# Four chunk pairs by seven products, one ReLU for a score pair, and a few squares and one form moved

## The chip, the cores and the metric

The kernel runs on one core of one Trainium2 chip. The core has a matrix engine (TensorE, called PE in the profile), a vector engine (VectorE, DVE), a scalar engine (ScalarE, ACT), GpSimd (POOL) and SyncE (SP), which here only issues DMAs. PE writes its results to PSUM, eight banks of 128 x 512 float32 values; ACT and DVE carry them from there to SBUF, the main on-chip memory. The metric is the device time of one execution in microseconds (us), as the median of several runs.

## The reference

Two computations follow each other. Attention without a softmax, over 8 batches of 3072 tokens, model width 256, key width 64:

```python
scores = (1.0 / S) * np.matmul(z, z.transpose(0, 2, 1))
attn = np.maximum(scores, 0.0) ** 2
x = u * np.matmul(attn, v)
```

Then a feed-forward part ("ff" below) on all 24576 tokens, with inner width 1024:

```python
h1 = x @ w1
h2 = x @ w2
out = np.maximum(h1, h2) @ w_out
```

The score matrix is symmetric, since queries and keys are the same z. In the ff, max(h1, h2) = relu(h1 - h2) + h2, so the kernel needs one inner product with the difference w1 - w2, a ReLU, and one linear term x @ (w2 @ w_out), whose matrix it works out once (`W2o_sb`).

## The kernel before, in words

**Tiling.** The 3072 tokens of a batch are 24 tiles of 128, in 6 groups of 512. Two groups make a couple, so a batch has 3 couples (c = 0, 1, 2). Scores are held in bf16 blocks of 512 x 512 (`Block`, `blk` in the profile). Only blocks on and above the diagonal are computed; the others are made by DMA transposes on SP (`mirror`, line 289, and for the blocks on the diagonal line 271). DMA transposes also turn z and u (lines 170, 220).

**Scores.** `score_pair` (from line 229) computes two tiles at a time: two matmuls of 64 rows each, side by side on the two row halves of PE (line 244), into two PSUM banks. Each half leaves its bank by a ReLU of 128 x 512 on ACT (line 258). Some steps later `finish` squares the pair, 128 x 1024, on DVE (line 268) or on ACT (line 266). Blocks on the diagonal of later batches ("triangles") are computed only from the diagonal on and squared half by half (line 264). A list of numbers in the loop over couples says which pairs of a couple ACT squares; the last two pairs of most couples are `late`: their squares wait for a Q token of the ff that follows, on ACT.

**Attention by seven products.** For a couple, attention times v is a product of 2 x 2 blocks of blocks. It is done by a scheme with seven products instead of eight (`product`, line 1202 for the matmuls), whose left factors are sums and differences of score blocks ("forms", 128 x 2048 each, DVE, line 343) and whose right factors are sums and differences of v tiles (`vt`, lines 200 to 203). The products run in two lanes, one on each row half of PE, 84 steps for a couple. Where an accumulator passes from one half to the other, a no-operation on POOL relays the semaphore. The score pairs of the next couple are spread between the steps (`at_step`), 14 for a couple.

**Feed-forward by seven products.** After the attention of couple i comes the ff of couple i-1 (`ff_by_seven`; plain `ff` for the first two couples). The 1024 inner columns are 8 chunks of 128. Chunk n and chunk n + 4 with the two token groups again make a 2 x 2 product. Three of the four pairs (x, y, z) take seven products P1 to P7 (line 607), with forms of the weights (`wT_sb`) and of the tokens (`token_forms`, lines 521 to 524); the fourth pair of chunks is done plainly (N tokens, line 569, two matmuls for each chunk and group). P1 is copied: where a bank is idle that was last filled whole, ACT copies it into a second PSUM bank (line 611) and P2 adds to it there ("seeded"; then a ReLU on ACT, line 582, makes the result); where not, to SBUF (line 615), and the sum is made by a custom operation on DVE that adds and clips (line 619). P6 and P5, which add up in P1's bank, are copied to SBUF (line 615); P3 leaves by a ReLU, P7 and P4 by the custom operation.

**What sets the order.** Each engine runs its own instructions in the order of the program. The order of an ff is written out by hand as a string of tokens (`FF_ORDER`, `FF_ORDER_MID` for c = 1 of batches 1 to 6, `FF_ORDER_LAST`): P1x is a product, N10 a plain chunk, O0z1 the outer product of group 0 with chunk z1 (four matmuls of 256 columns, line 552), L0a half of the linear term (four as well), E0 the way out of group 0 (line 649), Q a late square, T the next of the tasks handed over: a sum left from attention, and the forms for the next attention, two for each block of the couple, in the order of the blocks. A task's place in the string is thus its place in DVE's queue. Four PSUM banks (`mm0` to `mm3`) serve scores and inner products in turn (`idle_banks`), four are accumulators.

Of the kernel before, what the change touches and what calls it, by code (L numbers as in the profile page):

```python
# [12 lines left out]
def kernel(  # L13
# [10 lines left out]
    nc = tc.nc  # L24
    fp32 = mybir.dt.float32
# [33 lines left out]
    gpool = ctx.enter_context(tc.tile_pool(name="gpool", bufs=8))  # L59
    opool = ctx.enter_context(tc.tile_pool(name="opool", bufs=4))  # L60
    mm_psum = ctx.enter_context(tc.tile_pool(name="mm_psum", bufs=1, space=bass.MemoryType.PSUM))
    acc_psum = ctx.enter_context(tc.tile_pool(name="acc_psum", bufs=1, space=bass.MemoryType.PSUM))

# [3 lines left out]
    idle_banks = [f"mm{n}" for n in range(4)]  # L67
# [3 lines left out]
    def mm_tile(shape, dtype, name, hold=False, seeded=False, full=False):  # L71
        tag = next((t for t in idle_banks if t in whole), None) if seeded else idle_banks[0]
        if tag is None:
            return None, None
        idle_banks.remove(tag)
        if not hold:
            idle_banks.append(tag)
        if not seeded:
            (whole.add if full else whole.discard)(tag)
        return mm_psum.tile(shape, dtype, name=name, tag=tag), tag  # L80
# [149 lines left out]
    def score_pair(b, g, m, dve_half=None, halves=False, act=False):  # L230
# [8 lines left out]
        s_ps = []  # L239
        for h in range(2):  # L240
            rows = ds(h * R, R)
            q = z_at(b, g * G, h)
            s_ps.append(mm_tile([P, GW], fp32, "s_ps", full=not lo[h])[0])
# [9 lines left out]
        for h in range(2):  # L253
            s, o = s_ps[h][:, lo[h] :], r[:, tiles[h] - k, lo[h] :]
            if h == dve_half:
                nc.vector.tensor_single_scalar(out=o, in_=s, scalar=0.0, op=ALU.max)  # L256
            else:
                nc.scalar.activation(o, s, AF.Relu)  # L258
# [211 lines left out]
    def gate(b, g, hs):  # L470
# [13 lines left out]
    NP = 3  # L484
    FORM_CHUNKS = tuple((n, KF // 2 + n) for n in range(NP))
    PLAIN_CHUNKS = tuple(n for n in range(KF) if n not in sum(FORM_CHUNKS, ()))
    FF_ORDER = (
        "T P1z T N10 N11 L1a P6z P2z L0b N01 T O11 P5z T P1x O0z1 N00 P3z O10 P2x L0a P7z P1y O0z2 P6x O00 T P6y P4z P2y O01 P5x P5y P7x O1z1 P7y P3x Q O0x1 P3y T O1z2 P4y O1x2 O0x2 O0y1 P4x O0y2 O1y2 O1y1 O1x1 L1b Q E0 E1 T"
# [3 lines left out]
        "T T P1x T N00 T N10 T L0a P6x P1z L1a P2x L0b T P5x O00 P2z O0x1 P6z T N01 P7x P3x O10 P5z T P1y O0z1 O0x2 P3z O1x2 T T P6y T P4x T P2y N11 O01 P5y P7z P7y O0y1 O1x1 T Q P3y O0z2 O11 P4y P4z O1y2 Q O0y2 T E0 O1z2 O1y1 O1z1 T T T L1b T T E1"  # L492
# [34 lines left out]
    def ff_by_seven(b, c, tasks, last=False):  # L527
# [3 lines left out]
        homes = [Block() for n in range(3)]  # L531
# [760 lines left out]
```

## Time and profile before

| what | value |
|---|---|
| median of 3 runs | 894.4 us (892.91 to 895.82) |
| the profiled execution | 894.84 us |
| its span, first to last instruction | 892.8 us |
| TensorE's granted clock | 0.999 |
| PE busy | 885.2 us, 99% |
| DVE busy | 764.9 us, 86% |
| ACT busy | 735.4 us, 82% |
| POOL busy | 97.7 us, 11% |
| mean share of DMA engines on the hardware queue q1 | 73.9% |
| attention's matmuls (line 1202) | 2144 + 1560, 376 ns each |
| products in the ff (lines 607 and 569) | 379 ns each |

Lengths of single matmuls overlap: PE starts the next long before one has ended, so counts times lengths exceed the span. The span is 0 to 892.8 us; a row such as "213.74 0.39 PE L607 ..." starts at 213.74 us and lasts 0.39. In brackets stands how long the engine had been idle and what ended the wait. L607 is line 607 of the kernel before. In a table by stage each row is one stretch of the span; behind the bar of each engine stand its busy time and number of instructions, and at the end the granted clock and the load of the DMA engines.

### The profile page before, as it was taken

The page shows a single profiled execution, that of the slowest core. Times are in us where ns is not written, and L with a number is a line of the kernel's source. Part 1 is how long each engine was busy: PE and PEld are TensorE (multiplying, and loading weights), DVE is VectorE, ACT ScalarE, POOL GpSimd, SP SyncE. Part 2 cuts the span into 40 slices and gives each one's busy share as a digit, 9 for nine tenths or more (in the row PEclk, how much of TensorE's full clock was granted, in tenths as well). Part 3 has the DMA queues.
Part 4 walks back from the last instruction along what each step waited for, and adds up shares of the span by engine and source line. Part 5 has one row for each costly group of instructions (what it writes and reads, how often), then busy time and mean ns, then how long its engine had stood idle before and what let it go on. Part 6 is the DMA issues. An engine that isn't in the chain of part 4 may idle for free.

```text
span 892.8 us, 19566 instructions
## 1 busy us (share of the span) xinstructions
PE 885.2 (99%) x7458; PEld 505.5 (57%) x7458; DVE 764.9 (86%) x1201; ACT 735.4 (82%) x1366; POOL 97.7 (11%) x176
## 2 busy tenths in 40 slices
PE   9999999999999999999999999999999999999997
PEld 4555555565565555655656556566465564655655
DVE  6897887889988899798998899988898889987755
ACT  7978888788888888888888889888889888894554
POOL 3222100111002010020101101011100110000000
PEclk9999999999999999999999999999999999999999
DMA  9999999989899889998999999999989999998302
GB/s 179 250 224 197 201 198 146 205 145 197 168 178 185 175 139 161 191 151 165 173 168 203 153 183 160 149 198 134 212 150 144 189 134 205 144 150 158 80 1 95
DMA packets 396014, 148.10 MB, mean 166 GB/s; under 512 B 361264, under 2 KB 375856, under 8 KB 395920
## 3 DMA queue, kind: packets, MB, share of 16 engines
q1 hardware_dynamic: 373488, 119.32, 73.9%
q0 software_dynamic: 22288, 27.40, 22.6%
q8 instruction: 58, 0.95, 0.4%
q14 instruction: 36, 0.29, 0.1%
q10 hardware_dynamic: 144, 0.13, 0.0%
HBM read 59.77 MB, written 25.17 MB: 95 GB/s over the span
## 4 chain that ended last, share of the span: by engine, by line
PE 98%; DVE 1%; DMA 1%; issue 0%; ACT 0%; DVEq 0%
PE acc L1202 45%; PE acc L552 21%; PE d_ps L607 11%; PE s_ps L244 7%; PE acc L305 4%; PE d_ps L569 4%; PE acc L733 2%; PE d_ps L711 2%; DMA blk<-blk 1%; PE acc L892 0%; PE tpz L129 0%; DVE h_sb L1097 0%; PE w2o_ps L1000 0%; PE acc L675 0%; DVE blk L268 0%
## 5 line engine op out<-in xcount | busy, mean ns | idle before, releaser
L1202 PE MATMUL acc<-blk,v_sb 64*128 64x512 bf16 x2144 | 386.9, 376 | 0.0
L258 ACT ACTIVATE blk<-s_ps 128x512 bf16<-128x512 f32 (+1 forms) x584 | 287.4, 554 | 62.9 <-PE s_ps L244 60.5
L343 DVE TENSOR_TENSOR blk<-blk,blk 128x2048 bf16<-128x2048 bf16 x260 | 313.0, 1220 | 18.4 <-DMA blk<-blk 11.4
L1202 PE MATMUL acc<-blk,vt 64*128 64x512 bf16 x1560 | 316.3, 376 | 0.0
L1202 PEld LDWEIGHTS <-v_sb 64*128 64x128 bf16 x2144 | 152.0, 94 | 126.0 <-issue 5.0
L552 PE MATMUL acc<-w_out_sb,g_sb 128*128 128x256 bf16 x1400 | 190.3, 273 | 0.0
L552 PEld LDWEIGHTS <-g_sb 128*128 128x128 bf16 x1400 | 136.9, 98 | 56.1 <-DVE g_sb L619 0.6
L1202 PEld LDWEIGHTS <-vt 64*128 64x128 bf16 x1560 | 123.8, 94 | 75.5
L582 ACT ACTIVATE g_sb<-d_ps 128x512 bf16<-128x512 f32 x212 | 120.1, 600 | 9.0 <-PE d_ps L607 7.8
L244 PE MATMUL s_ps<-zT 64*128 64x512 bf16 (+3 forms) x672 | 125.5, 357 | 0.5 <-DVE r_sb L256 0.3
L619 DVE CUSTOM_DVE_ANT_0 g_sb<-blk,d_ps 128x512 bf16<-128x512 f32 x133 | 88.7, 684 | 36.4 <-PE d_ps L607 23.7
L268 DVE TENSOR_TENSOR blk<-blk 128x1024 bf16<-128x1024 bf16 x134 | 89.2, 686 | 19.9 <-ACT blk L258 19.9
L266 ACT ACTIVATE blk<-blk 128x1024 bf16<-128x1024 bf16 x78 | 82.3, 1055 | 0.9
L615 ACT COPY blk<-d_ps 128x512 f32<-128x512 f32 x133 | 76.6, 588 | 6.7 <-PE d_ps L607 3.7
L1097 DVE TENSOR_TENSOR h_sb<-h_sb,acc 128x512 f32<-128x512 f32 x89 | 58.9, 684 | 24.0 <-PE acc L1202 16.0
L186 POOL DMA_DIRECT2D v_sb<-in_v_dram x90 | 48.5, 557 | 272.6 <-PE acc L1202 216.5
L607 PE MATMUL d_ps<-blk,wT_sb 128*128 128x512 bf16 x198 | 68.4, 379 | 0.3 <-DVE g_sb L619 0.3
L473 DVE SCALAR_TENSOR_TENSOR xT<-h_sb,uT 128x512 bf16<-128x512 f32 x96 | 61.3, 689 | 2.1 <-DMA uT<-un 2.1
L649 ACT COPY o_sb<-acc 128x512 f32<-128x512 f32 x86 | 48.2, 587 | 14.5 <-PE acc L552 12.0
L244 PEld LDWEIGHTS <-zT 64*128 64x128 bf16 x672 | 35.7, 94 | 37.6 <-issue 0.4
L1101 ACT COPY h_sb<-acc 128x512 f32<-128x512 f32 x66 | 38.9, 590 | 19.3 <-PE acc L1202 17.8
L611 ACT COPY d_ps<-d_ps 128x512 f32<-128x512 f32 x65 | 37.8, 581 | 16.9 <-PE d_ps L607 16.9
(91 smaller groups left out, 782.4 us busy)
## 6 DMA issues: line engine op xcount, KB each, us to landing
out_dram<-o_sb SPq DMA_DIRECT2D x95, 256.0 KB, 3.0
un<-in_u_dram POOLq DMA_DIRECT2D x44, 256.0 KB, 5.3
v_sb<-in_v_dram POOLq DMA_DIRECT2D x84, 128.0 KB, 6.6
blk<-blk SPq DMA_TRANSPOSE x240, 5.1
zn<-in_z_dram POOLq DMA_DIRECT2D x18, 128.0 KB, 4.7
blk<-in_u_dram SPq DMA_DIRECT2D x4, 512.0 KB, 4.5
v_sb<-in_v_dram POOLq DMA_DIRECT2D x6, 256.0 KB, 6.2
blk<-in_moe_w_dram SPq DMA_DIRECT2D x2, 512.0 KB, 4.3
```

The source lines that it names most:

```text
L244: nc.tensor.matmul(s_ps[h][:, lo[h] :], zT[rows, z_at(b, blk * G + tiles[h], h), :], zT[rows, q + lo[h] // P : q + G, :].rearrange("p t c ...
L258: nc.scalar.activation(o, s, AF.Relu)
L266: nc.scalar.activation(both, r, AF.Square)
L268: nc.vector.tensor_mul(both, r, r)
L343: op(*((by_key(x) if mixed else x.ap) for x in blocks))
L473: lambda dc=dc: nc.vector.scalar_tensor_tensor(out=x[:, dc, :].rearrange("p (t r) -> p t r", r=P), in0=hs[dc].rearrange("p (t r) -> p t r" ...
L552: nc.tensor.matmul(o_ps[key][:, t % 2, :], x[:, ts(t, P)], w, start=first, stop=not left[key] and t % 2 == 1, skip_group_check=last,)
L582: nc.scalar.activation(g, ps, AF.Relu)
L607: nc.tensor.matmul(ps, w, x, start=first, stop=ends, skip_group_check=True)
L615: nc.scalar.copy(u_[k, name], ps)
L619: nc.vector._custom_dve(TENSOR_ADD_SAT, out=g, in0=u_[k, with_], in1=ps, s0=float("inf"), s1=0.0)
L1202: mm = nc.tensor.matmul(a.out(acc[name]), w()[rows], a.moving(rows, j), start=first, stop=left[name] == 0, skip_group_check=True,)
```

## The change

- All four chunk pairs (x, y, z, w) of an ff can take seven products (`NP = 4`). `FF_ORDER`, the string of 15 ffs, does so; `FF_ORDER_MID` and `FF_ORDER_LAST` keep the fourth pair plain. `FF_ORDER_MID` has the same kinds of tokens as before in another order.
- A new token p is a P1 that isn't seeded, even where a bank would be free: its copy goes to SBUF. The new `FF_ORDER` has p for x and y and P for z and w. It has six T instead of seven and one Q instead of two.
- In couples' attention the four PSUM banks are opened as two tiles of two banks (`mm_double`), in the ff as four of one (`mm_single`); the pools are closed and opened at each change. A score pair that is no triangle leaves its two-bank tile by one ReLU of 128 x 1024.
- The last of the tasks for couples c = 1 and 2 (one form) goes from the ff to step 0 of the attention that follows (`opening`).
- Only the last pair of a couple is late, except for c = 2; other pairs are squared on ACT.
- The pool for g has seven buffers instead of eight; the last ff takes its g tiles from idle blocks. The weight forms are 512 columns wide instead of 384.

```diff
-    gpool = ctx.enter_context(tc.tile_pool(name="gpool", bufs=8))
+    gpool = ctx.enter_context(tc.tile_pool(name="gpool", bufs=7))
...
+    def mm_pool(name):
+        mm_stack.close()
+        pool = mm_stack.enter_context(
+            tc.tile_pool(name=name, bufs=1, space=bass.MemoryType.PSUM)
+        )
+        mm_pools[:] = [name, pool]
+        n = 1 if name == "mm_single" else 2
+        for at in range(0, 4, n):
+            pool.tile([P, n, GW], fp32, name=f"{name}{at}", tag=f"{name}{at}")
...
+    def mm_pair(lo):
+        if mm_pools[0] == "mm_single":
+            return [mm_tile([P, GW], fp32, "s_ps", full=not x)[0] for x in lo]
+        first = idle_banks[0] // 2 * 2
+        for bank, x in zip((first, first + 1), lo):
+            idle_banks.remove(bank)
+            idle_banks.append(bank)
+            (whole.discard if x else whole.add)(bank)
+        return mm_pools[1].tile([P, 2, GW], fp32, name="s_ps", tag=f"mm_double{first}")
...
-        for h in range(2):
-            s, o = s_ps[h][:, lo[h] :], r[:, tiles[h] - k, lo[h] :]
-            if h == dve_half:
-                nc.vector.tensor_single_scalar(out=o, in_=s, scalar=0.0, op=ALU.max)
-            else:
-                nc.scalar.activation(o, s, AF.Relu)
+        if s_ps is not two and dve_half is None and not triangle:
+            nc.scalar.activation(r, two, AF.Relu)
+        else:
+            for h in range(2):
+                s, o = s_ps[h][:, lo[h] :], r[:, tiles[h] - k, lo[h] :]
+                if h == dve_half:
+                    nc.vector.tensor_single_scalar(out=o, in_=s, scalar=0.0, op=ALU.max)
+                else:
+                    nc.scalar.activation(o, s, AF.Relu)
...
-    NP = 3
+    NP = 4
     FORM_CHUNKS = tuple((n, KF // 2 + n) for n in range(NP))
-    PLAIN_CHUNKS = tuple(n for n in range(KF) if n not in sum(FORM_CHUNKS, ()))
+    PLAIN_CHUNKS = FORM_CHUNKS[-1]
     FF_ORDER = (
-        "T P1z T N10 N11 L1a P6z P2z L0b N01 T O11 P5z T P1x O0z1 N00 P3z O10 P2x L0a P7z P1y O0z2 P6x O00 T P6y P4z P2y O01 P5x P5y P7x O1z1 P7y P3x Q O0x1 P3y T O1z2 P4y O1x2 O0x2 O0y1 P4x O0y2 O1y2 O1y1 O1x1 L1b Q E0 E1 T"
+        "P1z p1y L0a P2y P6z L1a P6y P2z P5z T L0b P5y P7z O0y1 O0z1 P7y P3z P3y P4z O1z2 T P4y p1x O1y2 P1w O0y2 P6x O1z1 P6w T P2x O0z2 P5x P2w T O1y1 P5w O0x1 P7x P3x P7w O0w1 P3w P4x Q O0x2 P4w O1w2 O0w2 O1x1 E0 O1x2 O1w1 T L1b T E1"
     )
 
     FF_ORDER_MID = (
-        "T T P1x T N00 T N10 T L0a P6x P1z L1a P2x L0b T P5x O00 P2z O0x1 P6z T N01 P7x P3x O10 P5z T P1y O0z1 O0x2 P3z O1x2 T T P6y T P4x T P2y N11 O01 P5y P7z P7y O0y1 O1x1 T Q P3y O0z2 O11 P4y P4z O1y2 Q O0y2 T E0 O1z2 O1y1 O1z1 T T T L1b T T E1"
+        "T T P1y N00 N01 L1a P2y O00 P1z P6y O01 N10 T P6z T L0a P5y T L0b P2z T P5z T T P7z O10 T P3y T P1x O0y1 O0z1 O0y2 T P3z P4z P6x P2x O1z2 O0z2 T P7y P5x N11 P7x Q O1z1 P3x O0x1 O11 T P4x O1y2 P4y T O0x2 Q T T E0 T O1x2 O1x1 O1y1 T T L1b E1"
     )
...
-            if name == "P1":
-                seed, tag = mm_tile([P, GW], fp32, "d_ps", hold=True, seeded=True)
-                if tag:
-                    acc[k, "b"], bank[k, "b"] = seed, tag
+            if name == "P1" and seeded:
+                seed, at = mm_tile([P, GW], fp32, "d_ps", hold=True, seeded=True)
+                if seed is not None:
+                    acc[k, "b"], bank[k, "b"] = seed, at
...
+            elif kind == "p":
+                part("P1", token[2], seeded=False)
...
+            mm_pool("mm_double")
...
-            events = {}
+            events = {0: opening}
+            opening = []
...
-                    late = b and (c == 0 or b < B - 1) and n >= n_pairs - 2
-                    emit_pair(wait=6, act=late or b and n in ((0, 3, 6, 9), (0, 6), (6,))[c], late=late)
+                    late = b and (c == 0 or b < B - 1) and n >= n_pairs - (2 if c == NC - 1 else 1)
+                    emit_pair(wait=6, act=late or b and n in ((0, 6, 8), (0, 6, 7), (2, 6, 10))[c], late=late)
...
                 tasks = early + last_v
+                if b and c < NC - 1:
+                    opening = [tasks.pop()]
...
+            mm_pool("mm_single")
             second(i - 1, tasks, **({} if b else {"order": (2, 3, 0, 1)}))
```

## The prediction

> **What bounds the kernel now.** I read, in this order, the busy shares, a table by stage, TensorE's (PE's) timeline across a seam, and the waits.
>
> ```profile
> PE 885.2 (99%) x7458; PEld 505.5 (57%) x7458; DVE 764.9 (86%) x1201; ACT 735.4 (82%) x1366; POOL 97.7 (11%) x176
> ```
>
> PE is idle for only 7.6 of 892.8 us. A busy matmul row need not mean that PE moves at its best pace, so the stages must be looked at one by one (attention, ff, and so on in turn; columns: length, then busy PE, weight load, DVE, ACT, POOL):
>
> ```profile
> 139.86:156.76 16.90, 15.41 (x111) 10.56 (x109) 12.70 (x15) 13.80 (x24) 0.00 (x0) 1.00 1.24 167
> 192.44:213.74 21.30, 21.30 (x198) 9.46 (x197) 18.62 (x27) 18.02 (x34) 1.58 (x4) 1.00 0.92 183
> 213.74:228.84 15.10, 15.10 (x112) 10.59 (x111) 14.50 (x23) 13.55 (x24) 1.07 (x3) 1.00 1.09 165
> 228.84:249.78 20.94, 20.94 (x198) 10.13 (x197) 20.26 (x38) 18.40 (x36) 2.12 (x4) 1.00 0.92 168
> 249.78:264.88 15.10, 15.10 (x112) 10.59 (x111) 12.91 (x16) 13.71 (x24) 1.06 (x2) 1.00 1.05 179
> 264.88:285.50 20.62, 20.62 (x198) 10.61 (x197) 17.37 (x36) 16.29 (x35) 5.38 (x10) 1.00 1.15 195
> ```
>
> Every ff lasts 15.10 us; only the first one by seven products (139.86) takes 1.80 more. The pace comes from PE's timeline (start, length, operation):
>
> ```profile
> 148.84 0.38 PE L607 MATMUL d_ps<-xT,wT_sb 128*128 128x512 bf16 x1 [1.22 <-DVE g_sb L619]
> ...
> 213.74 0.39 PE L607 MATMUL d_ps<-xT,w_sb 128*128 128x512 bf16 x1
> 213.97 1.03 PE L569 MATMUL d_ps<-xT,w_sb 128*128 128x512 bf16 x4
> ...
> 226.12 2.35 PE L552 MATMUL acc<-w_out_sb,g_sb 128*128 128x256 bf16 x20
> ```
>
> Four 512-column matmuls last 1.03 and one 0.38, so one follows another every 0.65/3 = 0.217 us; twenty of 256 columns give (2.35 - 0.27)/19 = 0.109. An ff has 21 + 8 of the first and 80 of the second: 29 x 0.216 + 80 x 0.109 = 15.0 of its 15.10 us. So PE truly sets the time: only fewer matmuls make an ff shorter, and a wait costs what it lasts beyond its spare time. DVE with 20.26 of 20.94 us (stage 228.84) has the least slack behind PE.
>
> **Fewer matmuls.** A form pair needs seven products for two chunks and both token groups; the plain way needs eight. With the fourth pair an ff drops from 21 + 8 = 29 to 28. New order strings apply to all ffs by seven but the last; the middle one (c = 1, batches 1 to 6: six ffs) still holds its N tokens, and so does the last. Of 22 by seven, 22 - 6 - 1 = 15 change, and the built program has 15 matmuls fewer, 7443. All lie on the path: 15 x 0.216 = 3.24 us.
>
> **What the fourth pair costs behind PE.** Before, such an ff evicts by 4 plain ReLUs, and for each of three pairs 5 ACT operations and 2 of DVE's custom sum: 19 and 6. After, the seeded pairs (w, z) keep 5 and 2, the unseeded (x, y) have 4 and 3: 18 and 10. ACT's pace is 0.49 (two ReLUs 1.08, one 0.60), DVE's sum 0.60 (two 1.28, one 0.68), a form 1.14 (two 2.36, one 1.22), an ACT square's row 1.06. One form (S3 of the last block pair) goes to the next attention, one late square goes from ACT, and a gate, today the ff's last DVE row, falls behind the seam. DVE: 12.91 + 4 x 0.60 - 1.14 - 0.60 = 13.6 of 14.88; ACT: 13.71 - 0.49 - 1.06 = 12.2. Both fit, so nothing is charged.
>
> **Order of the products.** Here little is left. In the new order the seed's chain is P1z, copy to the second bank, P6z into the first bank. Between the two matmuls PE has p1y, four 256-column matmuls and P2y: 0.23 + 0.43 + 0.44 = 1.10 us. The chain takes:
>
> ```profile
> 148.10 0.68 DVE L619 CUSTOM_DVE_ANT_0 g_sb<-blk,d_ps 128x512 bf16<-128x512 f32 x1
> ...
> 214.22 0.57 ACT L611 COPY d_ps<-d_ps 128x512 f32<-128x512 f32 x1 [0.59 <-PE d_ps L607]
> ```
>
> Matmul 0.39, then 0.09 until the copy starts (214.22 after 214.13), 0.57, and 0.06 to PE (148.84 after 148.78): 1.11. That is 0.01 late; 15 times 0.01 is 0.15 us. With all three roundings against it, 0.03 late and 0.45; with them for it, nothing. I take 0.15. Every other accumulator in the order has at least 0.03 us by the same rows.
>
> **Squares and form in attention.** By the stages' order DVE gains one pair square (0.60) at c = 0, form and gate (1.74) at c = 1, form and gate less two squares (0.54) at c = 2: 20.86 of 20.94, 19.1 of 20.62, 19.2 of 21.30. Only the first is near its end. Bounds: nothing if it keeps inside, 0.3 us in each of seven stages (2.1) if half of that square ends behind its reader. I take nothing: a sum that stays inside its stage costs PE nothing. The moved S3 is first read at its lane's step 14, 14 x 0.216 = 3.0 us into attention, and takes 1.14 from the start. Two small edits go with this: the weight forms widen from 384 to 512 columns, once (four DVE operations at some 0.07 us more, by their rows of 350 and 419 ns), and seven g buffers instead of eight: in the new order a buffer's last reader ends 2.1 us or more before its next writer is due, so no eviction waits for one.
>
> **One ReLU for two.** 212 pairs leave by one 128x1024 ReLU. No row has it; rows by width do:
>
> ```profile
> L258 ACT ACTIVATE blk<-s_ps 128x512 bf16<-128x512 f32 x464 | 250.4, 597 | 57.0 <-PE s_ps L244 55.2
> L258 ACT ACTIVATE blk<-s_ps 128x384 bf16<-128x384 f32 x40 | 19.7, 493 | 0.0
> L258 ACT ACTIVATE blk<-s_ps 128x256 bf16<-128x256 f32 x40 | 15.3, 383 | 0.0
> L258 ACT ACTIVATE blk<-s_ps 128x128 bf16<-128x128 f32 x40 | 11.2, 279 | 5.8 <-PE s_ps L244 5.3
> ```
>
> 106 ns for each 128 columns, so 597 + 4 x 106 = 1021 ns; two in a row last 1.08 to 1.09, which is the upper bound. I take the line, since it is the same operation from the same memory. Bounds and value lie off the path while ACT keeps up (at most 18.6 of 20.94 us).
>
> **The wait added.** Closing one PSUM pool and opening the other makes the first matmul of each ff wait for all the old pool's readers: for the last ReLU of attention; its own bank's reader, the first ReLU of the row at 211.03 below, has long ended (211.63). Everything of PE is queued behind it. Today:
>
> ```profile
> 211.03 1.09 ACT L258 ACTIVATE blk<-s_ps 128x512 bf16<-128x512 f32 x2 [0.42 <-PE s_ps L244]
> 212.54 1.08 ACT L258 ACTIVATE blk<-s_ps 128x512 bf16<-128x512 f32 x2
> ```
>
> The last pair begins at 212.54; one of 1.02 ends 213.56, of 1.09 213.63; with 0.06 to PE that is 213.62 or 213.69, and the first matmul starts 213.74. So 0.12 or 0.05 us are spare: nothing charged. The Trainium skill ("ScalarE: Activation LUTs", Rules for kernel authors) budgets about 0.3 us per ACTIVATE and 0.83 ns per element, an estimate of 1.15 us here, by which the ReLU would end 213.69, PE would be 0.01 late and 21 seams would cost 0.2. The trace disagrees on the fixed part: by that rule 512 columns take 0.72, and the row says 0.597. At the other seam the last ff evictions end over 1 us ahead of the first scores.
>
> **The stall at 148.** There DVE waits for a transposed block:
>
> ```profile
> 146.96 1.23 DVE L343 TENSOR_TENSOR blk<-blk,blk 128x2048 bf16<-128x2048 bf16 x1 [2.69 <-DMA blk<-blk]
> ```
>
> The sum behind it is late and PE loses 1.8. In the new order this form, the fourth task, comes behind 21 products and 40 matmuls of 256 columns, 21 x 0.216 + 40 x 0.109 = 8.9 us into the ff (148.8), when the block has landed: the stall goes. Late next is POOL. Its relays, which hand an accumulator from one row half to the other, are queued behind a load of u that waits for SP's transposes:
>
> ```profile
> 157.75 0.53 POOL L212 DMA_DIRECT2D un<-in_u_dram x1 [21.15 <-DMA uT<-un]
> 160.46 0.53 POOL L212 DMA_DIRECT2D un<-in_u_dram x1 [2.18 <-PE s_ps L244]
> ```
>
> The first relay is needed at step 18 plus some three score pairs, 21 x 0.216 = 4.5 us into attention: 161.3 today, just behind 160.99. Without the stall and a matmul the ff ends at 154.74 and the relay is due at 159.3, so PE would wait about 1.7. SP's and POOL's lists are unchanged in order, so nothing pulls those transposes ahead. Bounds: -1.8 and 0.3; I take 0.
>
> Sum: -3.24 + 0.15 = -3.1 us. The profiled execution took 894.84 us, span 892.8 and 2.0 around it; that gives 891.7. It stands 0.4 above the median of the three runs (894.4), and from that the forecast is 891.3.
>
> **Rivals.** (a) The stall at 148 goes for good: 894.4 - 3.1 - 1.8 = 889.5. Speaking for it: SP's transposes could start sooner when the blocks are ready sooner. Against: SP is busy without a break from 140 to 163. (b) The gain is eaten: the DVE stage of 20.86 us slips (2.1), or the seed chain loses 0.45 and other chains as much: 892.5 to 893.5. For it: spare times of 0.01 to 0.12 us where there were 0.12 and more. Against: these durations repeat within some 10 ns. (c) Slower: the wide ReLU. It delays every ff's first matmul, 21 seams, from 1.14 us on; at 1.29 the 3.1 are gone, at 1.42 the kernel is 2.7 slower, at 1.5 it takes 894.4 - 3.1 + 21 x 0.36 = 898.9. For it: no row reads two banks at once. Against: the straight line of four widths. That the change does not do what it says is excluded by the 15 missing matmuls.
>
> **Chances.** Mine 0.58 (its own range 890.5 to 892.0), (a) 0.14, (b) 0.18, (c) 0.10. The range leaves out (c) and the far ends: 889.0 to 893.8. About 0.3% (2.7 us, so below 891.7) can be told from no change in this kernel: of mine 0.45 falls below it, with (a) 0.59 faster; the rest of mine and most of (b) 0.29 the same; 0.12 slower.
>
> **What would show it.** 7443 matmuls; ff stages of 14.88 at the changed orders and 15.10 in the middle one; ACT rows of 128x1024 near 1.02 us; no PE wait on ACT at the seams; the first ff's stage near 14.9 and a PE wait on POOL of 1 to 2 us some 4.5 us behind it. Wrong it would be with an ff stage above 15.0 us, or with attention above 21.3.

## The result, and the profile after

The changed kernel takes 890.2 us (median of seven, 889.12 to 892.49), the kernel before 894.4 (892.91 to 895.82): a ratio of 0.9951, 95% interval 0.9936 to 0.9967. The profiled execution took 890.65 us with a span of 888.7, against 894.84 and 892.8. The forecast was 891.3, range 889.0 to 893.8.

First the page of the profile after: the busy shares, and the new row of one ReLU for a score pair (columns of the row: times, then busy us and mean ns of one, then idle time ahead and what ended it).

```profile
PE 879.2 (99%) x7395; PEld 505.8 (57%) x7443; DVE 796.7 (90%) x1256; ACT 723.2 (81%) x1144; POOL 100.6 (11%) x176
...
L277 ACT ACTIVATE blk<-s_ps 128x1024 bf16<-128x1024 f32 x212 | 214.3, 1021 | 32.0 <-PE s_ps L267 30.2
```

The weight loads count 7443 matmuls (48 matmul records are missing, which leaves small holes in PE's busy time). The wide ReLU lasts 1021 ns. Then the table by stage (length; busy PE, weight load, DVE, ACT, POOL; granted clock, DMA share, GB/s), from the attention stage at 119 us on, attention and ff in turn:

```profile
118.95:141.01 22.06, 21.54 (x197) 10.49 (x197) 21.85 (x40) 18.28 (x26) 2.66 (x5) 1.00 0.99 189
141.01:155.89 14.88, 14.78 (x107) 10.47 (x108) 13.74 (x19) 12.43 (x22) 0.00 (x0) 1.00 0.94 156
155.89:176.53 20.64, 20.64 (x197) 10.92 (x196) 19.11 (x38) 16.85 (x30) 3.72 (x7) 1.00 1.11 205
176.53:191.42 14.89, 14.79 (x109) 10.49 (x110) 13.49 (x18) 12.44 (x22) 2.65 (x5) 1.00 1.18 160
191.42:212.68 21.26, 21.26 (x198) 9.46 (x197) 19.20 (x27) 19.12 (x22) 1.58 (x4) 1.00 0.81 161
212.68:227.77 15.09, 14.98 (x109) 10.56 (x109) 14.61 (x23) 13.46 (x24) 1.07 (x3) 1.00 1.22 163
227.77:248.71 20.94, 20.94 (x197) 10.04 (x197) 20.71 (x39) 17.89 (x26) 2.43 (x4) 1.00 1.22 172
```

The changed ffs last 14.88 us instead of 15.10, the middle one 15.10 as before, and attention keeps its 20.64, 21.26 and 20.94. The first ff by seven products (141.01) has lost its stall: 14.88 instead of 16.90. But the attention stage ahead of it (118.95), 20.94 before, now lasts 22.06. By the prediction's own sign, attention above 21.3, that would speak against it; the second profile below shows whether it is the kernel's. PE's timeline shows where:

```profile
133.25 0.37 PE L1239 MATMUL acc<-blk,v_sb 64*128 64x512 bf16 x1 [0.43 <-DVE h_sb L1133]
```

DVE is late there; its timeline has, some 17 us earlier, a form that waited for a transposed block:

```profile
116.11 1.23 DVE L369 TENSOR_TENSOR blk<-blk,blk 128x2048 bf16<-128x2048 bf16 x1 [2.58 <-DMA blk<-blk]
```

In the first profile of before the same form waited almost as long, 2.55 us, but ran at 114.77, 1.3 us earlier, while the stage began at the same time (118.92).

POOL, which was to be late next, is not; the two loads of u in its timeline:

```profile
156.96 0.53 POOL L235 DMA_DIRECT2D un<-in_u_dram x1 [19.05 <-DMA uT<-un]
160.00 0.53 POOL L235 DMA_DIRECT2D un<-in_u_dram x1 [2.51 <-PE s_ps L267]
```

The second load leaves POOL free near 160.5. With 1.1 us lost at 133 the relay is due about 155.89 + 4.5 = 160.4: there is no wait to be seen.

The best ledger cuts the span at the start of the attention stage that follows the first ff by seven products. Behind that cut before has 892.8 - 156.76 = 736.0 us and after 888.7 - 155.89 = 732.8: 3.2 of the 4.1 us. Ahead of it 156.76 stands against 155.89: 0.9, of which the ff's missing matmul is 0.2. The part behind the cut repeats to 0.1 us in the two profiles of each of these two kernels; the part ahead does not, and most of the experiments are about it.

### The profile page after: what moved, and what is told of

Its sections match the earlier page's. It is cut to its first block, busy times and chain, and to the rows that moved or that the text cites. A ratio compares the mean times of both kernels' runs of the same rounds, so it can differ in the third digit from the quotient of the medians.

```text
span 888.7 us, 19366 instructions
## 1 busy us (share of the span) xinstructions
PE 879.2 (99%) x7395; PEld 505.8 (57%) x7443; DVE 796.7 (90%) x1256; ACT 723.2 (81%) x1144; POOL 100.6 (11%) x176
## 4 chain that ended last, share of the span: by engine, by line
PE 95%; DVE 3%; issue 1%; DMA 1%; ACT 0%; DVEq 0%
PE acc L1239 44%; PE acc L579 22%; PE d_ps L640 13%; PE s_ps L267 7%; PE acc L331 4%; PE acc L768 1%; PE d_ps L602 1%; PE d_ps L746 1%; DVE blk L369 1%; DMA blk<-blk 1%; DVE blk L294 1%; PE acc L927 0%; DVE xT L499 0%; DVE h_sb L982 0%; DVE blk L290 0%
## 5 line engine op out<-in xcount | busy, mean ns | idle before, releaser
L277 ACT ACTIVATE blk<-s_ps 128x1024 bf16<-128x1024 f32 x212 | 214.3, 1021 | 32.0 <-PE s_ps L267 30.2
L579 PE MATMUL acc<-w_out_sb,g_sb 128*128 128x256 bf16 x1344 | 182.5, 273 | 0.8
L579 PEld LDWEIGHTS <-g_sb 128*128 128x128 bf16 x1344 | 131.5, 98 | 53.0
L652 DVE CUSTOM_DVE_ANT_0 g_sb<-blk,d_ps 128x512 bf16<-128x512 f32 x187 | 123.1, 684 | 21.6 <-ACT blk L648 14.7
L648 ACT COPY blk<-d_ps 128x512 f32<-128x512 f32 x193 | 111.3, 590 | 16.8 <-PE d_ps L640 13.4
L615 ACT ACTIVATE g_sb<-d_ps 128x512 bf16<-128x512 f32 x149 | 86.7, 599 | 18.6 <-PE d_ps L640 15.3
L294 DVE TENSOR_TENSOR blk<-blk 128x1024 bf16<-128x1024 bf16 x129 | 86.0, 684 | 13.0 <-ACT blk L277 12.9
L292 ACT ACTIVATE blk<-blk 128x1024 bf16<-128x1024 bf16 x83 | 87.6, 1056 | 1.2
L640 PE MATMUL d_ps<-blk,wT_sb 128*128 128x512 bf16 x242 | 87.3, 379 | 0.0
L284 ACT ACTIVATE blk<-s_ps 128x512 bf16<-128x512 f32 (+3 forms) x160 | 61.2, 437 | 24.8 <-PE s_ps L267 24.5
L1133 DVE TENSOR_TENSOR h_sb<-h_sb,acc 128x512 f32<-128x512 f32 x89 | 58.7, 682 | 14.5 <-PE acc L1239 13.7
```

The costliest lines, as they stand in the source:

```text
L277: nc.scalar.activation(r, two, AF.Relu)
L292: nc.scalar.activation(both, r, AF.Square)
L294: nc.vector.tensor_mul(both, r, r)
L579: nc.tensor.matmul(o_ps[key][:, t % 2, :], x[:, ts(t, P)], w, start=first, stop=not left[key] and t % 2 == 1, skip_group_check=last,)
L615: nc.scalar.activation(g, ps, AF.Relu)
L640: nc.tensor.matmul(ps, w, x, start=first, stop=ends, skip_group_check=True)
```

## The experiments

The theory was: the gain is 15 matmuls on PE's path; the other edits lie beside PE; the early stall goes with the new order, and POOL's relay takes its place. Times are medians, with the range; "the changed kernel" beside them is the run of the next paragraph. The last eight runs were on three other chips, where the kernel before took 895.15, 895.76 and 894.48 us, against 895.61 on the chip of the first four; so times of different chips are compared no closer than 1 us.

**The changed kernel again.**

> The changed kernel a second time, with nothing edited, as the base that the other three are held against on the same chip, and for a second profile of its first 170 us. If the new stall of 1.1 us in the attention stage near 133 us belongs to the kernel, it is there again within 0.2 us; if it is an accident of when SP's transposed blocks land, it has another size or another place, and the 890.2 us of the first measurement move by about that much. The other ff stages must again last 14.88 and 15.10 us.

890.49 us (889.72 to 892.28), ratio to before 0.995 (0.9933 to 0.9968). The stages by the same view:

```profile
120.43:141.37 20.94, 20.94 (x198) 10.04 (x197) 19.05 (x36) 18.17 (x26) 2.66 (x5) 1.00 1.06 189
141.37:156.25 14.88, 14.88 (x110) 10.48 (x109) 13.49 (x18) 12.44 (x22) 1.06 (x2) 1.00 1.08 180
```

The stall at 133 is gone, though nothing was edited: it belongs to the execution, and attention above 21.3 was no sign against the prediction. Behind the cut: 889.0 - 156.25 = 732.75, as in the first profile.

**The old order of products, all else as changed.**

```
-        "P1z p1y L0a P2y P6z L1a P6y P2z P5z T ...
+        "T P1z T N10 N11 L1a P6z P2z L0b N01 T O11 P5z T ...
```

> The changed kernel with the order of products from before in the ffs: the fourth chunk pair is done plainly again, with eight products; wide ReLU, moved squares, moved form and pool switch stay. My theory (the gain is 15 matmuls of 0.216 us, all on the path): 3.2 us above the changed kernel, so about 893.4, the fourteen undisturbed ff stages back from 14.88 to 15.10 us, attention unchanged. Rival (a good part comes from the wide ReLU and the moved squares, or from the stall that went): at most 1.5 us above it. In the first ff by seven products the form comes early in this order, so the stall of some 1.8 us at 148 us may be back too: then 5 us above and not 3.2.

894.68 us (892.87 to 897.82); ratio to before 0.9999 (0.9983 to 1.0015). The fastest stands 3.15 us above the fastest of the changed kernel, the median 4.2.

```profile
139.55:154.65 15.10, 15.10 (x111) 10.59 (x110) 12.90 (x16) 12.81 (x23) 1.06 (x2) 1.00 1.10 180
154.65:175.27 20.62, 20.62 (x197) 10.61 (x197) 17.41 (x36) 16.85 (x30) 5.38 (x10) 1.00 1.09 202
175.27:190.37 15.10, 15.10 (x112) 10.59 (x111) 12.90 (x16) 12.82 (x23) 0.00 (x0) 1.00 0.77 124
```

Without the fourth pair the kernel is as slow as before. And with the old order there is no stall in the first ff (15.10): the order alone does not make it.

**The fourth pair alone.**

```
-            mm_pool("mm_double")
...
+                    late = b and (c == 0 or b < B - 1) and n >= n_pairs - 2
+                    emit_pair(wait=6, act=late or b and n in ((0, 3, 6, 9), (0, 6), (6,))[c], late=late)
...
-                if b and c < NC - 1:
-                    opening = [tasks.pop()]
```

> The changed kernel with only the fourth pair: two ReLUs for each score pair again, no pool switch at the seams, the squares and the form where they were before. My theory (only matmuls count, the companions lie beside PE): the same time as the changed kernel within 0.5 us, ff stages of 14.88 us, although DVE then has 12.91 + 4 x 0.60 = 15.3 us of work booked to the tightest ffs, more than they last. Rival (the companions are what lets the fourth pair fit): DVE is 0.4 us or more late in the ffs of c = 0 and c = 1, some 14 of them, and the kernel 3 to 6 us above the changed one, with PE waits on DVE's sums in ff or at the start of the attention behind.

Not everything goes back: the pool of single banks is still closed and opened ahead of each ff, and the seven g buffers and the new middle order stay.

890.61 us (889.33 to 896.06), ratio 0.9959 (0.9935 to 0.9983).

```profile
175.92:190.80 14.88, 14.88 (x111) 10.48 (x110) 13.49 (x18) 12.45 (x22) 0.20 (x1) 1.00 1.25 134
190.80:212.05 21.25, 21.25 (x197) 9.45 (x196) 20.23 (x29) 18.72 (x35) 1.58 (x4) 1.00 0.84 169
```

The ffs last 14.88 us without the wide ReLU and without the moved squares and form. DVE's surplus ends behind the seam, where DVE has 20.23 busy of 21.25; it pressed on PE in a single ff, at 498.9, which lasts 15.19, with PE waiting for DVE's sum. Behind the cut this kernel has 888.5 - 155.30 = 733.2 us: 2.8 of the 3.2 us of steady gain, and 0.3 of the rest is that one ff. So the steady gain is the fourth pair, nearly all of it. Four of the twelve times lie at 894.5 to 896.1; of the 38 times of the changed kernel and of its variants with earlier or later moves below, none is above 893.5. Those four executions have no profile, so that stays open.

**The weight forms early.** Four DVE operations move from behind the last plain ff into the attention before.

```
+                for n, do in enumerate(weight_forms()):
+                    at(68 + 5 * n, do)
...
-                for do in weight_forms():
-                    do()
```

> The changed kernel with the four weight forms, 1.9 us of DVE just ahead of the attention stage near 133 us, moved into the attention before. My theory (DVE is late there because a transposed block lands late and the weight forms come behind it; what is late next is POOL, whose relays stand behind loads of u): the stall of 1.1 us near 133 us goes, and PE waits for POOL's relay about 160 us for 0.6 to 1.2 us instead, so the time moves by less than 0.5 us. Rival (nothing is queued behind that stall): the 1.1 us are kept and the kernel takes 1.1 us less than the changed one.

890.75 us (889.30 to 893.50). In this profile SP was on time, there was no stall at 133 to take away, and POOL's loads of u came at 153 and 155. It tells nothing between the two.

**One block turned twice.** What had differed between the profiles with a stall and those without? SP's queue and POOL's, where each sends a piece of work about 126 us: SP turns a block, POOL sends four loads. In the first profile of before, SP's timeline (start, length, queue) and then POOL's:

```profile
126.37 5.49 SPq L289 DMA_TRANSPOSE blk<-blk  x1
```

```profile
125.56 1.05 POOL L159 DMA_DIRECT2D zn<-in_z_dram  x2 [22.80 <-PE s_ps L244]
```

SP comes 0.81 us behind POOL's first load, needs 5.49 us to issue the block, and the last of six small blocks behind it lands at 146.8; in the profile of the old order above SP came 1.75 us ahead, needed 3.14, and the last one had landed at 137.6. So SP was delayed on purpose:

```
-        nc.sync.dma_start_transpose(
-            t.ap.rearrange("p (k r) -> p k r", r=P), A[b, g, blk].ap
-        )
+        for n in range(2 if (b, g, blk) == (1, 2, 3) else 1):
+            nc.sync.dma_start_transpose(
+                t.ap.rearrange("p (k r) -> p k r", r=P), A[b, g, blk].ap
+            )
```

> The changed kernel, in which SP turns one block twice, ahead of the small blocks of the first triangle: everything behind it on SP's queue comes 7 to 11 us later. It shows what step 7 of the prediction spoke of, a late block in the first ff by seven products, on purpose. My theory: in the new order the form that needs the small blocks runs near 150 us, behind their landing near 147, so this ff still lasts 14.9 us; what is late next is POOL, whose relay for the attention behind stands behind two loads of u that wait for SP: these come about 162 and 164 us, the relay is due near 160.5, and PE waits there 3 to 5 us. The kernel is 3 to 5 us above the changed one. Rival (there is slack enough behind all of this): no wait of PE above 0.5 us and the same time as the changed kernel.

892.83 us (889.68 to 901.78). The last small block landed at 145.5. The ff and the attention behind it, by the view of stages:

```profile
140.21:155.09 14.88, 14.88 (x110) 10.47 (x108) 13.48 (x18) 12.43 (x22) 0.00 (x0) 1.00 0.83 139
155.09:176.98 21.89, 21.25 (x197) 11.86 (x196) 19.16 (x38) 16.94 (x30) 3.71 (x7) 1.00 1.10 207
```

PE's timeline in that attention:

```profile
160.65 0.39 PE L1240 MATMUL acc<-blk,v_sb 64*128 64x512 bf16 x1 [0.64 <-POOLq L1249]
```

The ff keeps its 14.88, and PE waits for POOL's relay: the stage behind lasts 21.89 instead of 20.62. The mechanism is as expected; its size is 1.3 us, not 3 to 5, since the last small block came 6 us later than in the changed kernel again (139.55) and not 7 to 11, and POOL's second load of u started at 160.50 and not near 164. Three of the ten executions took 898 to 902 us, two of them with a mean granted clock of 0.995, as after the long waits of the next two kernels; they were not profiled, so the margin of the new order is shown for the profiled execution and not for every one.

**The same delay in the old order.**

> The same second turn of one block, in the changed kernel with the old order of products (the fourth pair plain). My theory: here the form is due near 144 us and the small blocks land near 147, so DVE waits about 3 us, PE about 2 us near 148, and this ff lasts some 17 us as in the first profile of before; POOL's relay near 161 then costs 1 to 3 us, since the ff's own wait has taken the rest. Against the kernel with the late block in the new order it is 3.2 us slower (the 15 matmuls) and not 5, because the two waits stand in a row and only the later one counts. Rival (the ff's wait comes on top): 5 us or more between the two.

897.57 us (894.05 to 907.90). In the profiled execution (span 900.4) SP also fell behind POOL's loads, by 1.71 us, and the last small block landed at 150.3. DVE's timeline shows the form that waited for it; it was due at 150.48 - 4.96 = 145.52, 4.6 us into the ff:

```profile
150.48 1.22 DVE L370 TENSOR_TENSOR blk<-blk,blk 128x2048 bf16<-128x2048 bf16 x1 [4.96 <-DMA blk<-blk]
```

The ff, cut into pieces by the view of stages (the granted clock is the third number from the end):

```profile
140.90:148.40 7.50, 7.50 (x52) 5.01 (x52) 4.58 (x6) 6.76 (x13) 0.00 (x0) 1.00 0.51 99
148.40:152.30 3.90, 0.28 (x2) 0.00 (x0) 1.82 (x3) 0.83 (x2) 0.00 (x0) 0.89 0.57 109
152.30:154.00 1.70, 1.65 (x6) 0.86 (x6) 1.70 (x2) 0.60 (x1) 0.00 (x0) 0.50 1.13 207
154.00:156.00 2.00, 2.00 (x9) 0.97 (x7) 0.39 (x2) 1.07 (x2) 0.00 (x0) 0.50 1.38 68
156.00:158.00 2.00, 2.00 (x9) 1.14 (x8) 1.41 (x3) 0.76 (x2) 0.00 (x0) 0.50 1.24 273
158.00:160.00 2.00, 2.00 (x17) 1.46 (x16) 1.43 (x2) 1.27 (x2) 0.00 (x0) 0.94 1.14 211
```

PE stands for 3.8 us; and then the granted clock is 0.50 for about 6 us, in which a 512-column matmul follows the last after 427 ns instead of 216. The ff lasts 21.83, 6.7 more than without: 3.8 of waiting, 2.9 of half speed. After the wait of 1.22 us in the first profile of before the clock stayed at 1.00. POOL's relay then costs nothing (the next attention lasts 20.62), so of these two waits only the earlier counted; both numbers expected, 17 us for the ff and 1 to 3 us at the relay, are missed. And the lateness reached further: the second ff by seven products, at 183.3, lasts 16.67 instead of 15.10, again behind a form that waited for a turned block (2.42 us, until 196.56). The landings of the two kernels differ by 4.8 us, so their times can't be set against each other; the due time can, 4.6 us into the ff here against 9.3 in the new order (149.54 in the kernel of the paragraph above, whose ff began at 140.21).

**Three turns in the new order**, with 3 in place of the 2 in the last diff.

> The changed kernel in which SP turns the one block three times: the small blocks then land near 150 us, as late as in the old order with its late block (150.05 us), where PE lost 6.7 us in the first ff by seven products. My theory (in the new order the form that reads them is due near 150.3 us instead of 144): this ff lasts 14.9 us, at most 1.5 more, and the wait comes behind it: POOL's relay near 160 us, with loads of u near 163 and 165, 4 to 6 us. Rival (the order gives no such margin): 18 us or more in this ff.

901.64 us (894.51 to 906.99). The last small block landed later than was meant, at 155.1; DVE's timeline:

```profile
155.18 1.22 DVE L370 TENSOR_TENSOR blk<-blk,blk 128x2048 bf16<-128x2048 bf16 x1 [3.96 <-DMA blk<-blk]
```

The form was due at 151.22, 9.4 us into the ff. PE waited 3.9 us, then ran at a clock of 0.50 for some 5 us, and the ff lasted 21.38; the next attention waited for POOL's relay and lasted 22.71. The number expected for the ff is missed, because the blocks came 5 us later than planned; the margin that it was to show, 4.8 us more than in the old order, is there.

**The seed chain.** P6z comes closer to P1z:

```
-        "P1z p1y L0a P2y P6z L1a ...
+        "P1z p1y P2y P6z L0a L1a ...
```

> The changed kernel with four matmuls of 256 columns moved from before P6z to behind it, in the changed order strings: between P1z and P6z PE then has 0.66 us of work instead of 1.10, and the work as a whole is the same. My theory (the chain of matmul, copy and hand-over takes 1.11 us by the rows of before): each of the 15 ffs gets 0.45 us longer, 15.3 us, with PE waiting on ACT's copy; 6.7 us in all. If the chain is really shorter than the 1.10 us that PE has in the changed kernel (no wait was seen there), this ff shows by how much: an ff of 15.2 us means a chain of 1.0 us. Rival (the copy starts before the matmul's end as the profile models it, so nothing was ever near): ffs of less than 15.1 us.

896.22 us (894.94 to 900.76). The changed ffs last 15.27, 0.39 more, and PE's list of waits names the copy (us in total, times, longest):

```profile
PE d_ps L640 <- ACT d_ps L644: 3.2, 14, 0.3
```

The copy in ACT's timeline:

```profile
249.47 0.57 ACT L644 COPY d_ps<-d_ps 128x512 f32<-128x512 f32 x1 [0.59 <-PE d_ps L640]
```

The products around it in PE's (the first row begins with P1z, the second is P6z):

```profile
249.04 0.82 PE L640 MATMUL d_ps<-xT,w_sb 128*128 128x512 bf16 x3
250.09 0.38 PE L640 MATMUL d_ps<-blk,wT_sb 128*128 128x512 bf16 x1 [0.23 <-ACT d_ps L644]
```

The chain is 250.09 - 249.04 = 1.05 us: 0.43 until the copy starts, 0.57, 0.05 to PE. The changed order leaves 1.10, so 0.05 are spare. The ratio to before is 1.0018: the 15 times 0.39, 5.9 us, undo all of the gain.

**The last score pair later.** Its step is one later:

```
-                at_step.setdefault(2 + n * (len(steps) - 2) // max(n_pairs, 1), []).append(n)
+                at_step.setdefault(2 + n * (len(steps) - 2) // max(n_pairs, 1) + (b > 0 and n == n_pairs - 1), []).append(n)
```

> The changed kernel with the last score pair of each attention one step, 0.216 us, later. My theory of the added wait (the ff's first matmul waits for the last ReLU, which has 0.12 us to spare): the margin is overdrawn by 0.10 us at some 21 seams, 2.1 us in all, with PE waits on the wide ReLU at the seams. If the margin is 0.05 us, 3.5 us. Rival (the first matmul doesn't wait for the last ReLU, or it has far more to spare): no change within 0.5 us and no such waits.

893.54 us (892.06 to 894.93). The attention stages last 20.72, 21.36 and 21.04, each 0.10 longer, to the hundredth what was worked out. The sum is smaller: behind 194 us, where nothing else differs from the changed kernel again, it is 1.5 us over 17 such seams (2.1 over 21 was expected), since most ffs get 0.01 shorter and two stages near the end don't lengthen. At a seam, the last ReLU in ACT's timeline:

```profile
250.49 1.02 ACT L277 ACTIVATE blk<-s_ps 128x1024 bf16<-128x1024 f32 x1 [0.23 <-PE s_ps L267]
```

The first products of the ff in PE's:

```profile
251.57 0.59 PE L640 MATMUL d_ps<-xT,w_sb 128*128 128x512 bf16 x2
```

The ReLU ends at 251.51 and the ff's first matmul starts at 251.57, although its own bank was free long ago: the wait on the pool is real, and the changed kernel has 0.11 us to spare for it. (PE's list of waits doesn't name it: the modelled end of the matmul ahead, 251.53, leaves only 0.04 us of idle time.) This profile also held an early execution of the other kind, which nobody had arranged: SP's block 1.36 us behind POOL's loads, 6.24 us to issue, the last small block at 147.5, later than in the first profile of before. The ff lasted 14.87, and the attention behind it 21.94 instead of 20.72, with PE waiting for POOL's relay.

**Before again.** No edit.

> The kernel before a second time, for another profile of its first 170 us. My theory: the stall of 1.8 us at 148 us belongs to the executions in which SP reaches the block near 126 us only after POOL's four loads near 125 us (0.8 us behind them in the first profile of before: 5.5 us to issue, 16.4 until it landed). So if SP is ahead of those loads here, the first ff by seven products lasts 15.1 us and the span is 1.5 to 2 us shorter than 892.8; if it is behind them, the stall is there again. Rival (the stall belongs to the old order): 16.9 us in this ff whichever of the two comes first.

893.3 us, a single execution, span 891.3. SP's timeline, POOL's, and the stages:

```profile
125.51 3.37 SPq L289 DMA_TRANSPOSE blk<-blk  x1
```

```profile
125.85 1.06 POOL L159 DMA_DIRECT2D zn<-in_z_dram  x2 [22.80 <-PE s_ps L244]
```

```profile
119.21:140.15 20.94, 20.94 (x197) 10.04 (x197) 19.29 (x37) 18.66 (x36) 2.66 (x5) 1.00 1.13 192
140.15:155.25 15.10, 14.99 (x109) 10.58 (x110) 12.90 (x16) 13.71 (x24) 1.06 (x2) 1.00 1.08 176
```

SP is 0.34 us ahead of POOL this time, and the ff lasts 15.10. Behind the cut: 891.3 - 155.25 = 736.05, as in the first profile.

**POOL's loads later**, by twelve small memsets:

```
+            if (b, c) == (1, 0):
+                for n in range(12):
+                    at(24, nc.gpsimd.memset, behind, 0.0)
...
-                        at((62 if b == 1 else 44) + 12 * piece, turn_z, b + 1, piece)
+                        at((68 if b == 1 else 44) + 12 * piece, turn_z, b + 1, piece)
```

> The changed kernel, in which POOL clears a small tile twelve times (some 2.7 us by the 223 ns of its one such row) ahead of the four loads near 125 us, and turns two pieces of z six steps later. My theory: SP's block near 126 us is then always ahead of these loads, is issued in 3 to 4 us and lands within 10, also where SP is late; then no execution waits for the small blocks or for POOL's relay, the upper half of the times comes down and the median falls by up to 0.7 us; the stages behind 157 us don't change. Rival (the spread of 889 to 892.5 us comes from earlier, or from elsewhere): times and spread as in the changed kernel. A loss: if z lands too late for DVE, PE waits 1 us or more near 137 us.

890.74 us (889.81 to 891.24, six times). The block took 3.17 us to issue and 5.1 to land, the shortest of all, but SP was on time in this profile anyway. The median did not fall; the highest time is lower, with too few to tell.

**All early moves together**: the weight forms early, POOL's loads later, and two loads of u moved behind the relay:

```
-            if b and c < 2:
+            if b and c < 2 and (b, c) != (1, 0):
...
+            elif (b, c) == (1, 1):
+                at(19, load_u, b, q1)
+                at(20, load_u, b, q2)
+                at(50, turn_u, b, q1)
+                at(56, turn_u, b, q2)
```

> The last kernel with two further moves in the early part: the four weight forms in the attention before, and the two loads of u that stand ahead of POOL's relay near 160 us behind it instead. My theory: with all three of the waits seen in the first 165 us taken away, the early part is as short as the shortest seen, and the median is 1 us below the changed kernel, about 889.3 us, with a spread below 1.5 us. Rival (the rest of the spread comes from the first 118 us, which none of the three touches): no change beyond 0.3 us.

889.9 us (889.47 to 891.13, six times; 889.3 was expected), ratio to before 0.9937 (0.9917 to 0.9958). In its profile SP reached the block at 129.1, as late as in any other, yet still ahead of POOL's loads (129.7; 2.7 us earlier without the memsets, and then SP would have been 2 us behind), and none of the three stages had a stall: 20.94, 14.88, 20.62. The interval overlaps that of the changed kernel, so a version that is surely faster than both was not found. What spread is left fits the first 118 us, as the rival had it, but six times and one profile don't show it: the attention stage at 119 began between 118.6 and 121.0 in the fourteen profiles.

The early part in all profiles (block: issue behind POOL's first load; length of the issue; time to landing, of the first turn where there are several; then the lengths of the attention stage at 119, the ff and the attention behind it, which with the last pair later are 0.10 longer for that reason):

```
kernel                     behind   issue  landing  attention  ff      attention
before                     +0.81    5.49   16.35    20.94      16.91   20.62
changed                    +1.87    7.47   10.86    22.07      14.88   20.64
last pair later            +1.36    6.24   15.54    21.39      14.87   21.94
old order, late block      +1.71    7.32   11.57    21.86      21.83   20.62
three turns                +1.88    7.34   10.77    22.19      21.38   22.71
before again               -0.34    3.37    9.26    20.94      15.10   20.62
changed again              -1.65    3.13    7.42    20.94      14.88   20.62
old order                  -1.75    3.14    6.95    20.94      15.10   20.62
fourth pair alone          -0.49    3.37    8.88    20.94      14.88   20.62
weight forms early         -1.46    4.23    9.79    20.94      14.88   20.62
late block                 -2.05    3.74    9.06    20.94      14.88   21.89
seed chain                 -1.42    3.04    7.69    20.94      15.27   20.62
loads later                -4.36    3.17    5.13    20.94      14.88   20.62
all early moves            -0.65    3.65    9.61    20.94      14.88   20.62
```

Every execution with the block behind the loads lost time in one of the three stages; of those with it ahead only the one that was delayed on purpose did, apart from the 0.39 us that the seed chain's edit costs.

## Why the prediction was right, and where not

**Fewer matmuls: right.** 7443 matmuls, 15.10 to 14.88 in every changed ff. Undoing this alone returns the time of before, doing it without the wide ReLU and the moved squares and form gives the changed kernel's median. Behind the cut the gain is 3.2 us, of which fourteen ffs make 14 x 0.22 = 3.1; an ff near the end that had lasted 15.20 gave the other 0.1. With the first ff it is 3.4 where 3.24 was worked out.

**Evictions, squares and form: right, and hardly needed.** DVE has 13.5 to 13.7 of 14.88 in the changed ffs (13.6 was worked out), ACT 12.4 (12.2), and DVE in attention 20.71, 19.11 and 19.20 (20.86, 19.1, 19.2). But the fourth pair alone has the same median: the moves protect something that DVE's slack in attention protects already, but for 0.3 us in one ff. Whether they keep the highest times down, four of twelve without them, is open.

**The seed chain: sized wrong.** The term 1.11 us is 1.05; its hand-over from the matmul's end to the copy, 0.09, is 0.04 to 0.05. The row was read rightly: in both profiles of before the copy at a seam starts 0.48 us after the start of its matmul, at 20 and 19 seams. In the changed kernel it starts after 0.43, at 19 seams, and so it does with the old order of products and with the fourth pair alone; what in these kernels shortens it stays open. The 0.15 us charged is nothing.

**The wide ReLU: right to the ns**, 1021. The estimate by the Trainium skill ("ScalarE: Activation LUTs", Rules for kernel authors), 1.15 us, is too high here; the page states that rule for a bias passed as a pointer operand, and the kernel passes this ReLU no bias. Two banks in one read cost nothing extra: 1021 ns lies on the line of the one-bank widths.

**The added wait: right.** The margin of 0.12 is 0.11 by the kernel with the last pair later (0.22 less the 0.10 that it lost).

**The stall at 148 and POOL behind it: wrong in the cause of the first half; the sum is not contradicted.** The prediction took the stall for a property of the old order. The stall came and went with SP's lateness, without an edit, and a delay of SP on purpose brought such waits in either order; the old order reads the small blocks 4.6 us into the ff and then pays for it, the new one reads them at 9.3. That half of the step, "comes behind ... when the block has landed", holds: with the last one at 147.5 the new order still lost nothing. So does "late next is POOL": 1.2 us in the kernel with the last pair later, 1.3 in the delayed one, against 1.7 worked out. In the profile after, it did not show only because another 1.1 us had been lost at 133, which the prediction did not see: the same lateness of SP, through DVE's form at 116 and the weight forms behind it. This fits the three other profiles in which SP came 1.4 us or more behind the loads (21.39 to 22.19 there), and the one with all early moves, where the weight forms come earlier: SP was later still, and that stage stayed at 20.94.

On the early part as a whole, "net 0" is not contradicted: the cut comes at 156.76, 155.25 and 154.65 in the three undelayed profiles of the old order, mean 155.6, and at 155.89, 156.25, 155.30, 155.68, 155.52 and 156.21 in six of the new, mean 155.8 (156.0 with the kernel with the last pair later, at 157.27, of which 0.1 is its edit). The shorter ff alone would put the new ones 0.2 earlier. With points ahead that move by 2.4 us so few profiles can't tell 0 from some 1 us either way.

**Why 890.2 and not 891.3.** The sum is right to 0.3 us: 3.1 was forecast, and 3.4 are measured with the first ff, half of the difference being the seed chain's 0.15. The fastest times of the two kernels on one chip (893.05 of thirty, 889.72 of seven) are 3.3 us apart. The median of 890.2 lies 0.3 below the range given for the main line alone (890.5 to 892.0), and nearer to rival (a)'s 889.5 than to 891.3. The medians are 4.2 to 5.1 apart, because the times of before reach higher (to 900.9 there). That the old order pays for late blocks which the new one covers fits this, and the old order with all else changed has the same high times; but the high executions were not profiled, and the fourth pair alone has four of them too. One sign is on record: of the 85 executions of before beside the later runs five show a mean granted clock of 0.995 to 0.997, and all five took 897.6 us or more, while the changed kernel's fourteen all show 0.999 or 1.0. In the two kernels with the long waits such a mean (0.995) came from half speed behind a wait, so at least these five fit a long wait of PE somewhere. Most of the high times have no such mark. So this last us is argued and not shown. Of the rivals, (a) is what the profile after shows at 148 and not what the early part gives on the mean; (b) and (c) had no part.

## What to carry to other kernels

Where one engine is busy 99% of the time and its pace repeats to 0.01 us, count its instructions: the gain is their number times their pace, and the edits that make room on the other engines need a test of their own, for they may be worth next to nothing in the median. Cut the span where it begins to repeat, and compare the parts: here 3.2 us lay behind the cut, to 0.1 in both profiles of each of the two kernels, while a point ahead of all changed ffs moved by 2.4 us. A wait seen in one profile is not yet a property of the kernel; a second profile of the same program costs less than a theory.

## What was not expected of the hardware

What a transfer of SP beside POOL's loads costs went with its place among them: the same transpose of a 512 x 512 block (128x2048 in SBUF) took 3.0 to 4.2 us to issue and 5 to 10 to land in the nine profiles with it ahead of the four loads, 5.5 to 7.5 and 11 to 16 in the five with it behind them. Only one profile parts this place from SP's lateness, that of all early moves: SP as late as ever but ahead of the loads, 3.65 and 9.61. So 2.9 us at the issue of the block (126.4 in the first profile of before, 123.5 in that of the old order) became 9.2 us at the last small block (146.8 and 137.6). What makes SP late by these first 2 or 3 us, in some executions and not in others, was not found.

A wait of PE beyond some length is paid twice. In the two kernels with the longest waits PE lost 3.8 and 3.9 us by standing still. By the clock record of their traces the granted clock fell to 0.50 some 2.8 and 2.2 us after the end of the last matmul and stayed there for 6.83 us in both; PE worked for 5.9 and 5.3 us of that, which added 2.9 and 2.6 us. After waits of 1.5 us and less (three turns in the new order at 169.6, the first profile of before) it stayed at 1.00. The Trainium skill ("TensorE: Matmul & The Clock Gate", Part 1) puts the idle window that brings half the clock at about 3.4 us, and the lengths of the waits agree with that, though the clock fell sooner behind the last matmul; for the way back it names about 3.4 us of sustained work, and here it took 5.9 and 5.3.
